# Two pairs of heads take turns in the products of probabilities and values

## The chip, the cores and the metric

One core of one Trainium2 chip runs the whole kernel in one launch. The metric is the device time of that launch in microseconds (us): 900.86 us is the median of 3 runs (900.86 to 901.72).

## The reference

Attention over 4 batches, 8 heads, 576 positions and a head dimension of 64, in float32, and then two gated layers. Heads 0 to 3 of each batch see the last 32 positions, heads 4 to 7 see every fourth of the last 128:

```python
scores = np.where(masks, scale * q @ k.T, -1e9)       # window 32, or 128 with step 4
attn = softmax(scores)
x = (attn @ v) as rows of 2304 tokens x 512           # 8 heads x 64
x = (sigmoid(x @ w_gate) * (x @ w_val)) @ w_out       # 512 -> 1536 -> 512
h = x @ w_in                                          # 512 -> 2048
out = (max(h, 0) + alpha * min(h, 0)) @ w_out2        # 2048 -> 512
```

## The kernel before, in words

**Blocks of heads.** The four heads of one kind in one batch make a block `hb` (0 to 7). They lie on the 128 partitions as two *pairs*: pair 0 on partitions 0 to 63, pair 1 on 64 to 127, 32 partitions for each head. The dilated heads are reordered by the host, so that both kinds become a band of windows of 32 positions: queries of window n need keys of windows n-1 and n.

**A product of probabilities and values** (`pv_mm`, L423 to L441) is computed for half of a block's 18 windows at a time. A matmul contracts over the 64 partitions of one pair: the weights are the values of one window (64 partitions x 128 columns, two heads beside each other), and what streams is the transposed probabilities of the one or two windows of queries that need them (64 or 32 columns). Both operands are split in a high and a low half in float16, and `passes` (L482) gives three matmuls for each window: high x high, high x low, low x high. The first half has 9 windows of keys, so 27 matmuls for each pair (24 with 64 columns and 3 with 32); the second half has 10, so 30 (24 and 6). Every matmul is compiled to a weight load of its own and the matmul. Each pair accumulates in a PSUM bank of its own, which `att_bank` gives. Block 0 takes another way (`pv32_mm`, L453, in float32, with 32 rows for each matmul), so seven blocks use `pv_mm`: 7 x 114 = 798 matmuls.

**What follows** is `pv_x` (L460): for each pair ScalarE reads the bank and writes the high half of `xh`, the input of the gate and value products, and VectorE writes the low half.

**Order of the work.** All instructions stand in an order written by hand, and each engine works through its own list in that order. The first batch, together with the decoding of the weights (VectorE, L179 to L187) and their powers of two (`total_of`, a matmul with one column, L148, then VectorE L156 and L160, then GpSimd L164), is a script of tasks, `FIRST`. In it `pvm hb half` is `pv_mm`, `pvx` is `pv_x`, `dec m` decodes, `wb m` bounds and `wsum m` sums a block of weights, `g b m` and `v b m` are the gate and value products (L590), `spl` splits weights. The parts around the first two uses are

```
pvm 1 1 4; pvm 1 0; dec 1; pvx 1 1 1; pvx 1 0 0; lgv 3; spl 0 1 1; pvx 1 1 0; g 0 0 0; wb 1; wsum 1; ... wpow 1
sig 0 7; pvm 2 0; wpow 9; v 0 7 1; spl 9 0; g 0 8 0; dec 10; ... pvx 2 0 0; ... g 0 8 1; wb 10; wsum 10
```

From then on a loop over batches runs the gate and value products of batch b (`gv_mm`, 12 blocks m of 128 columns) and its output products (`o1_mm`, L632), and `attention(b + 1)` hangs the next batch's attention on fixed places of that loop: block 2b at m = 7 and 8, block 2b + 1 in the output products (places 14 and 15). `prepare` fits the steps that prepare the second layer's weights (VectorE, ScalarE, GpSimd and transfers) between them. The gate and value products rotate through three buffers of two PSUM banks; ScalarE (L603) and VectorE (L608) empty them. After the attention comes the second layer (L964, L1207), whose weights went through memory in the meantime.

Of the kernel before, what the change touches and what calls it, by code (L numbers as in the profile page):

```python
# [17 lines left out]
WINDOW = 32  # L18
# [6 lines left out]
def attention_moe_kernel(  # L25
# [26 lines left out]
    H2 = S // 2  # L52
# [46 lines left out]
    def hold(bank, key):  # L99

        assert holds.get(bank) not in open_ and holds.get(bank) not in waiting, (bank, holds[bank], key)
        holds[bank] = key
# [18 lines left out]
    def att_bank(key, spare=None):  # L121
        if spare is None:
            turn["a"] = (turn["a"] + 1) % 2
            spare = 6 + turn["a"]
        hold(spare, key)
        waiting.add(key)
        return banks[:, spare, :]
# [264 lines left out]
    def pieces_of(hb):  # L392
        ends = [0, 352, 736, NB * 64] if hb < 2 else [0, NB * 64]
        return list(zip(ends[:-1], ends[1:]))

    def p_half(hb, z, c0, c1):
        for a, e in pieces_of(hb):
            if a <= c0 < e:
                assert c1 <= e
                o = 2 * a + z * (e - a) + c0 - a  # L400
                return st_[hb][0].bitcast(F16)[:, o:o + c1 - c0]
# [14 lines left out]
    xt = {}  # L416
    plain_v = set()

    def pv(hb, half):
        pv_mm(hb, half)  # L420
        pv_x(hb, half)

    def pv_mm(hb, half, spare=None):  # L423
        b, kind = divmod(hb, 2)
        v_ = vh[hb]
        first, last = (0, NB // 2) if half == 0 else (NB // 2, NB)
        ops = [(m, max(m, first), min(m + 2, last)) for m in range(max(first - 1, 0), last)]
        tiles = []
        for pair in range(2):
            k = slice(64 * pair, 64 * pair + 64)  # L430
            ps = att_bank(("pv", hb, half, pair), None if spare is None else spare + pair)[:, :H2]
            tiles.append(ps)
            for z, (m, n0, n1) in enumerate(ops):
                p_ = [p_half(hb, i, WINDOW * (m + n0 + 1), WINDOW * (m + n1 + 1))[k] for i in range(2)]
                w = [v_[k, i, m].rearrange("p h d -> p (h d)") for i in range(2)]
                for i, (a, x_) in enumerate(passes(w, p_)):
                    nc.tensor.matmul(  # L437
                        ps[:, WINDOW * (n0 - first):WINDOW * (n1 - first)], lhsT=a, rhs=x_,
                        start=(z == 0 and i == 0), stop=(z == len(ops) - 1 and i == 2), skip_group_check=True,
                    )  # L440
        xt[hb, half] = tiles  # L441

    def pv32_mm(hb, half, spare):

# [33 lines left out]
    def passes(w, x_):  # L478
        return ((w[0], x_[0]), (w[0], x_[1]), (w[1], x_[0]))
# [765 lines left out]
    def part(i):  # L1245
# [21 lines left out]
        "vhi": v_hi,  # L1267
        "vlo": v_lo,
        "pvm": pv_mm,
        "pv32": pv32_mm,  # L1270
        "pvx": pv_x,
# [33 lines left out]
    with tc.manual_schedule():  # L1305
# [66 lines left out]
        for n in range(2 * KD):  # L1372
            c, h = n // 2, n % 2
# [134 lines left out]
        i = 2 * turn["m"]  # L1508
# [169 lines left out]
```

## Time and profile before

| | us |
|---|---|
| median of 3 runs | 900.86 |
| the profiled execution, its own time | 900.97 |
| its span on the core | 899.2 |
| TensorE busy (matmuls) | 850.2 (95%) |
| VectorE busy | 681.9 (76%) |
| ScalarE busy | 450.4 (50%) |
| GpSimd busy | 304.6 (34%) |
| mean granted clock of TensorE | 0.967 of full speed |

The page of the profile gives busy times by engine, the span in 40 slices and the chain of work that ended last:

```profile
PE   7879789799999999999999989997899999999998
DVE  5999999825887767778695958678888888886751
PEclk9699689799999999999999999999999999999999
```

A digit is the busy share of one fortieth of the span (22.5 us) in tenths; PEclk is the granted clock in tenths. TensorE is busy throughout, but for the first eight slices, where VectorE is full, and a stretch after the middle. The 1.8 us by which the profiled time exceeds the span lie before the first and after the last instruction.

### The profile page before, as it was taken

The numbers are of one execution on the slowest core, as the hardware profiler recorded it, in microseconds if no ns is written. First come the engines' busy times: TensorE is split into PE (matmuls) and PEld (weight loads), VectorE is DVE, ScalarE is ACT, GpSimd is POOL, SyncE is SP. The second block draws the span as 40 slices with busy tenths as digits, with TensorE's granted clock in tenths as the row PEclk, the third lists the DMA queues.
The fourth block names the chain that finished last, engine by engine and source line by source line (L and its number), as shares of the span: only waits on it lengthen the run. The fifth ranks groups of instructions, "written<-read, shape, count | busy, mean of one in ns | idle before, by whom it ended". The sixth has DMA issues, their size and how long they took to land.

```text
span 899.2 us, 19438 instructions
## 1 busy us (share of the span) xinstructions
PE 850.2 (95%) x8196; PEld 701.5 (78%) x8196; DVE 681.9 (76%) x1039; ACT 450.4 (50%) x739; POOL 304.6 (34%) x264
## 2 busy tenths in 40 slices
PE   7879789799999999999999989997899999999998
PEld 5657567587787878777888768886788888888887
DVE  5999999825887767778695958678888888886751
ACT  4677556434453545343434556554565456545430
POOL 2456656600201101102024873245344454343220
PEclk9699689799999999999999999999999999999999
DMA  9764344104415425106756885954755685575462
GB/s 323 266 212 151 121 141 158 58 28 141 139 51 182 144 74 195 62 1 230 266 180 219 300 279 195 347 218 184 265 236 188 240 322 188 199 274 203 142 214 83
DMA packets 85176, 166.81 MB, mean 186 GB/s; under 512 B 5345, under 2 KB 57697, under 8 KB 85089
## 3 DMA queue, kind: packets, MB, share of 16 engines
q1 hardware_dynamic: 85088, 165.57, 52.5%
q8 instruction: 64, 1.05, 0.5%
q14 instruction: 24, 0.19, 0.1%
HBM read 137.24 MB, written 28.31 MB: 184 GB/s over the span
## 4 chain that ended last, share of the span: by engine, by line
PE 57%; DVE 26%; ACT 6%; issue 4%; DMA 4%; POOL 1%; SPq 1%; ACTq 0%; DVEq 0%; POOLq 0%
PE banks L590 14%; PE banks L1207 14%; PE banks L964 13%; PE banks L632 12%; DVE plain L183 4%; DVE plain L187 3%; PE banks L437 3%; DVE plain L179 2%; DVE temp_w L1010 2%; DVE temp_y L1010 1%; DVE gf L608 1%; DVE halves L824 1%; DMA words<-w_gate 1%; DVE g_gv L1049 1%; PE banks L323 1%
## 5 line engine op out<-in xcount | busy, mean ns | idle before, releaser
L590 PE MATMUL banks<-xh,w_gv 128*128 128x288 f16 x2304 | 297.7, 291 | 1.5 <-ACT sg L603 1.5
L590 PEld LDWEIGHTS <-w_gv 128*128 128x128 f16 x2304 | 226.1, 99 | 62.6 <-issue 1.8
L964 PE MATMUL banks<-yh,w_i 128*128 128x256 f16 x1536 | 189.9, 275 | 12.1 <-ACT temp_y L1019 6.4
L964 PEld LDWEIGHTS <-w_i 128*128 128x128 f16 x1536 | 151.3, 99 | 32.5 <-issue 12.3
L632 PE MATMUL banks<-gt,w_o 128*128 128x288 f16 x1152 | 149.5, 291 | 1.0 <-POOL gt L168 0.9
L632 PEld LDWEIGHTS <-w_o 128*128 128x128 f16 x1152 | 113.5, 100 | 31.9 <-issue 1.1
L1207 PEld LDWEIGHTS <-g_gv 128*128 128x128 f16 x780 | 76.7, 98 | 9.1
L1207 PE MATMUL banks<-w,g_gv 128*128 128x256 f16 x612 | 75.5, 273 | 0.0
L164 POOL TENSOR_SCALAR sc<-sc 128x1 f32<-128x1 f32 x35 | 12.4, 354 | 180.7 <-DVE sc L160 180.6
L1059 POOL TENSOR_TENSOR yh<-temp_y 128x512 f32<-128x512 f32 x16 | 27.0, 1689 | 131.6 <-DVE temp_y L1010 126.9
L194 ACT ACTIVATE junk<-plain 128x1024 bf16<-128x1024 f32 (+1 forms) x36 | 36.4, 1010 | 60.4 <-DVE plain L198 32.1
L1010 DVE SCALAR_TENSOR_TENSOR temp_w<-neg,sc,temp_w 128x256 f32<-128x256 f32 x48 | 55.5, 1195 | 10.9 <-ACT neg L1002 10.8
L187 DVE SCALAR_TENSOR_TENSOR plain<-words,plain 128x512 uint32<-128x512 uint32 x68 | 61.9, 931 | 1.2
L183 DVE SCALAR_TENSOR_TENSOR plain<-words,plain 128x512 uint32<-128x512 uint32 x68 | 59.3, 893 | 1.2
L1207 PEld LDWEIGHTS <-g_g 128*128 128x128 f16 x564 | 55.2, 98 | 6.4
L168 POOL TENSOR_TENSOR gt<-gf,gt 128x576 f16<-128x576 f32 x24 | 36.8, 1533 | 65.2 <-ACT gt L615 65.2
L608 DVE SCALAR_TENSOR_TENSOR gf<-banks,sg 128x576 f32<-128x576 f32 x48 | 36.0, 750 | 29.3 <-PE banks L590 28.9
L603 ACT ACTIVATE sg<-banks,sc 128x576 f32<-128x576 f32 x48 | 35.2, 734 | 35.1 <-PE banks L590 24.7
L615 ACT ACTIVATE gt<-gf 128x576 f16<-128x576 f32 x48 | 32.3, 675 | 38.3 <-DVE gf L608 38.3
L1207 PE MATMUL banks<-w,g_g 128*128 128x256 f16 x396 | 48.3, 273 | 0.0
L179 DVE TENSOR_SCALAR plain<-words 128x512 uint32<-128x512 uint32 x68 | 40.2, 612 | 8.9 <-DMA plain_dram<-plain 5.5
L388 POOL TENSOR_TENSOR s<-s,rs 128x1152 f32<-128x1152 f32 (+1 forms) x9 | 17.8, 1975 | 71.7 <-DVE rs L383 64.4
(170 smaller groups left out, 1300.1 us busy)
## 6 DMA issues: line engine op xcount, KB each, us to landing
w_i<-wi_dram SPq DMA_DIRECT2D x40, 896.0 KB, 6.4
w<-w_dram SPq DMA_DIRECT2D x52, 512.0 KB, 8.4
words<-w_out SPq DMA_DIRECT2D x28, 512.0 KB, 5.2
plain<-w_dram SPq DMA_DIRECT2D x18, 512.0 KB, 8.9
words<-w_in SPq DMA_DIRECT2D x16, 512.0 KB, 4.8
w_dram<-halves SPq DMA_DIRECT2D x28, 256.0 KB, 4.9
q<-qbd SPq DMA_DIRECT2D x6, 1152.0 KB, 6.5
words<-w_gate SPq DMA_DIRECT2D x12, 512.0 KB, 4.9
```

Source lines behind the costliest of these rows:

```text
L168: engine.tensor_tensor(out=lo, in0=src, in1=hi, op=ALU.subtract)
L179: nc.vector.tensor_scalar(out=d, in0=hi, scalar1=3, scalar2=0x3FFFFFFF, op0=ALU.logical_shift_left, op1=ALU.bitwise_and)
L183: nc.vector.scalar_tensor_tensor(out=d, in0=hi, scalar=0xC0000000, in1=d, op0=ALU.bitwise_and, op1=ALU.bitwise_or)
L187: nc.vector.scalar_tensor_tensor(out=d, in0=lo, scalar=29, in1=d, op0=ALU.logical_shift_right, op1=ALU.bitwise_or)
L194: nc.scalar.activation(junk[:, :src.shape[1]], src, AF.Square, accum_out=dst)
L590: nc.tensor.matmul(ps[:, h, :], lhsT=a, rhs=x_[:, H2 * h:H2 * h + H2], start=(kk == 0 and i == 0), stop=(kk == KD - 1 and i == 2),)
L603: nc.scalar.activation(halves(sg), ps, AF.Sigmoid, scale=sgx[b][:, m:m + 1])
L608: nc.vector.scalar_tensor_tensor(out=halves(gf), in0=ps, scalar=2.0 ** -15, in1=halves(sg), op0=ALU.mult, op1=ALU.mult)
L632: nc.tensor.matmul(ps[:, h, :], lhsT=a, rhs=x_[:, H2 * h:H2 * h + H2], start=(m == 0 and z == 0), stop=(m == M1 - 1 and z == 2),)
L964: nc.tensor.matmul(o, lhsT=h, rhs=l, start=(new and v == 0 and q == 1), stop=(q == total_), skip_group_check=True,)
L1010: nc.vector.scalar_tensor_tensor(out=temps[x_][:, c], in0=t[:, c], scalar=slope[:, u + v:u + v + 1], in1=src[:, c], op0=ALU.mult, op1=ALU.add,
L1207: nc.tensor.matmul(ps[:, H4 * t:H4 * t + H4].rearrange("p (c f) -> p c f", c=2), lhsT=a, rhs=x_, start=(first and k == 0 and t == 0 and z ...
```

## The change

Before, all matmuls of pair 0 of a half come first, then all of pair 1. After, the loop over pairs is the innermost: for each window and pass one matmul of pair 0 (rows 0 to 63 of the array) and then the same one of pair 1 (rows 64 to 127). Both banks are asked for at the start. The number, the operands and the order of the matmuls within a pair stay; so do the calls of `pv_mm` and of `pv_x`.

```diff
-        tiles = []
-        for pair in range(2):
-            k = slice(64 * pair, 64 * pair + 64)
-            ps = att_bank(("pv", hb, half, pair), None if spare is None else spare + pair)[:, :H2]
-            tiles.append(ps)
-            for z, (m, n0, n1) in enumerate(ops):
-                p_ = [p_half(hb, i, WINDOW * (m + n0 + 1), WINDOW * (m + n1 + 1))[k] for i in range(2)]
-                w = [v_[k, i, m].rearrange("p h d -> p (h d)") for i in range(2)]
-                for i, (a, x_) in enumerate(passes(w, p_)):
+        xt[hb, half] = [
+            att_bank(("pv", hb, half, pair), None if spare is None else spare + pair)[:, :H2] for pair in range(2)
+        ]
+        for z, (m, n0, n1) in enumerate(ops):
+            p_ = [p_half(hb, i, WINDOW * (m + n0 + 1), WINDOW * (m + n1 + 1)) for i in range(2)]
+            w = [v_[:, i, m].rearrange("p h d -> p (h d)") for i in range(2)]
+            for i, (a, x_) in enumerate(passes(w, p_)):
+                for pair, ps in enumerate(xt[hb, half]):
+                    k = slice(64 * pair, 64 * pair + 64)
                     nc.tensor.matmul(
-                        ps[:, WINDOW * (n0 - first):WINDOW * (n1 - first)], lhsT=a, rhs=x_,
+                        ps[:, WINDOW * (n0 - first):WINDOW * (n1 - first)], lhsT=a[k], rhs=x_[k],
                         start=(z == 0 and i == 0), stop=(z == len(ops) - 1 and i == 2), skip_group_check=True,
                     )
-        xt[hb, half] = tiles
```

## Rows read from the trace of the kernel before

**Rows 1.** The chain that ended last, page's part 4: shares of the span by engine

```profile
PE 57%; DVE 26%; ACT 6%; issue 4%; DMA 4%; POOL 1%; SPq 1%; ACTq 0%; DVEq 0%; POOLq 0%
```

**Rows 2.** Windows: stretch, length, busy (instructions) by engine, clock, DMA share, GB/s

```profile
0.00:175.35 175.35, 144.75 (x1482) 107.80 (x1482) 159.49 (x247) 106.92 (x193) 94.19 (x88) 0.86 0.55 183
175.35:437.80 262.45, 260.98 (x2759) 208.53 (x2760) 179.99 (x299) 118.61 (x170) 27.76 (x27) 0.99 0.35 118
```

**Rows 3.** All instructions of line 437: duration in ns, min/median/max

```profile
L437 PEld LDWEIGHTS <-vh x684: 92/95/129, 105.8 to 428.7; 64*128 64x128 f16 x171
L437 PE MATMUL banks<-s,vh x684: 172/190/239, 105.8 to 428.7; 64*128 64x64 f16 x150, 64*128 64x32 f16 x21
```

**Rows 4.** Windows of line 437 alone: PE, PEld busy, clock; four of 13 bursts

```profile
31.58:36.84 5.26, 5.26 (x112) 5.22 (x112) 0.50 0.91 303
...
105.77:108.46 2.69, 2.69 (x54) 2.65 (x54) 0.50 0.90 287
...
175.48:177.04 1.56, 1.56 (x54) 1.52 (x54) 1.00 0.05 11
...
427.14:428.85 1.71, 1.71 (x60) 1.67 (x60) 1.00 1.07 380
```

**Rows 5.** Timeline of PE, matmuls in flight in 116.60:116.70 and in 117.14:117.26

```profile
116.42 0.45 PE L437 MATMUL banks<-s,vh 64*128 64x64 f16 x10
...
116.97 0.46 PE L437 MATMUL banks<-s,vh 64*128 64x64 f16 x14
```

**Rows 6.** Timeline of PE, block 0's products, which alternate the pairs

```profile
16.82 2.12 PE L453 MATMUL banks<-pt,vc 32*64 32x64 f32 x72 [0.60 <-DVE mx L341]
```

**Rows 7.** Timeline of PE, one-column matmuls of L148; first and last of 23

```profile
461.19 0.24 PE L148 MATMUL banks<-sc,mask_sb 128*128 128x1 bf16 x4
...
461.75 0.16 PE L148 MATMUL banks<-mask_sb 128*128 128x1 bf16 x1
```

**Rows 8.** Timeline of PE, the first two matmuls of line 437

```profile
29.13 0.21 PE L437 MATMUL banks<-st_pt,second 64*128 64x32 f16 x2 [0.80 <-DVE xh L172]
```

**Rows 9.** Timelines of PE, DVE and POOL after block 1's products

```profile
36.84 3.06 PE L590 MATMUL banks<-xh,w_gv 128*128 128x288 f16 x12
...
38.03 0.81 DVE L172 SCALAR_TENSOR_TENSOR xh<-banks,xh 128x288 f16<-128x288 f32 x1
39.97 0.16 DVE L156 TENSOR_SCALAR sc<-banks 128x1 uint32<-128x1 uint32 x1 [1.13 <-PE banks L148]
...
34.05 1.64 POOL L168 TENSOR_TENSOR w_gv<-plain,w_gv 128x512 f16<-128x512 f32 x1 [1.45 <-ACT w_gv L205]
```

**Rows 10.** Timelines of PE and DVE after block 2's first half

```profile
108.46 6.41 PE L590 MATMUL banks<-xh,w_gv 128*128 128x288 f16 x36
...
114.96 0.16 DVE L156 TENSOR_SCALAR sc<-banks 128x1 uint32<-128x1 uint32 x1 [1.26 <-PE banks L148]
```

**Rows 11.** Timeline of PE after block 2's second half

```profile
130.76 0.48 PE L309 MATMUL banks<-mask_sb 128*128 128x384 bf16 x1 [3.83 <-DVE xh L172]
```

**Rows 12.** The chain in order of time: first and last of ten full-clock bursts

```profile
175.55 1.56 PE banks L437 x51
...
427.21 1.71 PE banks L437 x60
```

**Rows 13.** All of PE's waits in 175.4:437.8: total us, times, longest

```profile
PE banks L148 <- DVE sc L845: 2.5, 1, 2.5
PE banks L590 <- ACT sg L603: 1.5, 2, 1.2
```

**Rows 14.** Timeline of DVE: its last waits before the second layer's weights

```profile
447.83 0.43 DVE L179 TENSOR_SCALAR plain<-words 128x512 uint32<-128x512 uint32 x1 [3.26 <-DMA plain_dram<-plain]
...
461.49 0.76 DVE L608 SCALAR_TENSOR_TENSOR gf<-banks,sg 128x576 f32<-128x576 f32 x1 [0.26 <-PE banks L590]
```

**Rows 15.** Timeline of SP: transfers issued behind the last output product

```profile
439.16 0.34 SPq L652 DMA_DIRECT2D y_dram<-y  x1
```

**Rows 16.** Windows, as rows 2: the stretch behind block 3's first half

```profile
177.20:183.30 6.10, 6.10 (x40) 4.33 (x39) 1.44 (x2) 1.40 (x2) 0.00 (x0) 0.73 0.00 0
```

## The prediction

> **What bounds the kernel now.** I read the page's chain of waits first, then a table of windows by stage, then line 437 by itself, then timelines around each of its bursts. In the chain the reader is to see that TensorE holds 57% of it and VectorE 26% [rows 1]. The windows say where which one bounds. Up to 175.35 us VectorE is busy for 159.5 of 175.35 us and TensorE for 144.8; from there to 437.8 us TensorE is busy for 261.0 of 262.45 us and VectorE for 180.0 [rows 2]. The changed line has 13 bursts, one for each half of a block, save that block 1's two halves run as one behind a first two matmuls. Three of them lie in the first stretch (blocks 1 and 2), ten in the second (blocks 3 to 7), and all ten stand in the chain, the first and last as pieces of 1.56 and 1.71 us [rows 12]. So in the second stretch a microsecond taken from TensorE counts unless another engine falls behind; in the first it counts only as far as VectorE was waiting for it.
>
> **What one burst costs.** At full clock the burst of 54 takes 1.56 us and the one of 60 takes 1.71 us [rows 4]. The six more matmuls have 32 columns, so one of those costs 0.15 / 6 = 25 ns. Ten matmuls of 64 columns in flight start 0.45 - 0.19 = 0.26 us from first to last, nine steps of 29 ns [rows 3, 5]. One column in a cycle of 2.4 GHz would make 64 / 2.4 = 27 ns: the matmuls of one half of the rows already follow each other as fast as their columns stream, and the weight loads (busy beside them for 1.52 of the 1.56 us [rows 4]) cost nothing. No cost of loading goes away by the change; the only thing to gain is that two halves of the rows stream at once.
>
> **Do two halves stream at once?** The trace has a place where they do. In the middle of a burst the last three matmuls of pair 0 meet the first three of pair 1, all with 32 columns. There 14 matmuls start in 0.46 - 0.18 = 0.28 us [rows 5]. One after the other the 13 steps would be 7 x 29 + 6 x 25 = 353 ns. So some 73 ns are missing, three steps of 25 ns: three matmuls of one pair ran beside three of the other, each pair at its own step. Block 0's products alternate the same two halves, 32 rows at a time, and show no break between turns: 72 matmul records in 2.12 us, 29 ns each [rows 6].
>
> **The change part by part.** Nothing is added or removed: 798 loads and 798 matmuls stay, and no transfer moves. Block 1's opening needs the low half of the values for its third pass, as before; four matmuls instead of two go ahead of that wait. Both banks are needed at once, where pair 1's was needed half a burst later; its last reader is VectorE's `pv_x` of an earlier half, long past in every burst, so I cost that at nothing; if a bank were late, it would be by at most the 0.8 us that the half burst used to give. Pair 0's result used to be ready at half of the burst, and now is at the end of one that takes about half as long: nothing for `pv_x`.
>
> At full clock a burst of 54 becomes 27 steps: 24 x 29 + 3 x 25 = 771 ns. Before it was 48 x 29 + 6 x 25 - 75 = 1467 ns, and 1.56 us with the 0.09 us around it. The gain is 0.70 us. For 60: 24 x 29 + 6 x 25 = 846 ns against 1617 ns, a gain of 0.77 us. A block gains 1.47 us, and the five blocks in the second stretch 7.35 us. What may not pass this on: in that stretch TensorE waits for others for 2.5 us once, ahead of the first burst, and 1.5 us in two waits on ScalarE [rows 13]. The longer of these two is reached by a path over ScalarE and VectorE that itself starts at an earlier gate or value product, so it moves with TensorE. VectorE has 262.45 - 180.0 = 82 us idle there [rows 2], against 7 to take. Behind the stretch VectorE runs without idle time from 447.8 us, released by a transfer, to its 0.26 us wait for TensorE at 461.5 us [rows 14]. That would eat the gain if the transfer stood still; but transfers are issued in order, and SP sends the last output product first, at 439.2 us [rows 15], which TensorE finishes at 437.8. So it moves too. I count all 7.35 us.
>
> In the first stretch the clock is at half. Block 1 takes 5.26 us for 112 matmuls [rows 4]; half of it is 2.6 us saved on TensorE. Then come 12 gate products (3.06 us), the sum L148 and VectorE's reading of it at 39.97 us. VectorE was waiting for that for 1.13 us; without TensorE it would be ready at 38.03 + 0.81 = 38.84 us [rows 9]. TensorE's new date: the products need the low weights, which GpSimd ends at 34.05 + 1.64 = 35.69 us; four of the 12 don't, and eight at 0.255 us bring it to 37.7 us. VectorE is late next, and the gain is its 1.1 us. Block 2's first half takes 2.69 us at half clock [rows 4]: 1.3 us saved. 36 gate products in 6.41 us follow, and the sum for which VectorE waits 1.26 us [rows 10]. In these products the clock rises, about 3.5 us in (36 at 0.25 us, or at 0.124 us after the rise, make 6.2 us with 14 of the first kind). If it rises at the same time as before, five more of them run at half clock, 5 x 0.126 = 0.65 us; I count 0.65 us. Block 2's second half saves 0.77 us, which VectorE hides: the next thing of note on TensorE is 3.83 us of waiting for it [rows 11].
>
> The sum is 7.35 + 1.1 + 0.65 = 9.1 us. The profiled execution took 900.97 us by itself, so 891.9 us; against the median of 900.86 that is 9.0 us or 1.0%.
>
> **Bounds.** No row shows a long run of matmuls that alternate with 29 / 2 = 14.5 ns from start to start. The nearest from below is the meeting of the pairs (three steps hidden of three). From the other side are the one-column matmuls, 23 of them from 461.19 to 461.75 us, 25.5 ns each [rows 7], though these all use all rows. I take 14.5 ns, because the meeting is this very instruction on these halves. An exposed weight load is bounded by block 1's first two matmuls, which start 0.21 - 0.173 = 37 ns apart [rows 3, 8], 12 ns more than 25. The clock is one more term: after the idle time ahead of block 3 the next stretch ran at 0.73 of full speed for 6.1 us [rows 16], so 6.1 x 0.27 = 1.65 us were lost. Such a stretch may go or come where everything moves by some 2 us; I take none and keep 1.7 us either way.
>
> **Rivals.** *TensorE can't be fed that fast.* Matmul and load together are two instructions in 14.5 ns, and what ran so in the trace was short enough to have lain ready. If starts come 25 ns apart at best [rows 7], a burst of 54 takes 1.35 + 0.09 = 1.44 us and one of 60 takes 1.59: 0.12 us less in ten bursts, 1.2 us. Half clock is little touched (53 / 2 = 26.5 ns), so 1.75 us stay. 900.97 - 2.95 = 898.0 us. For it: no sustained row is faster than 25 ns. Against it: the meeting, which went at 12 ns for six matmuls. The Trainium skill, "TensorE: Matmul & The Clock Gate", section "Wait — 56ns, not 53.3ns?", states it as a rule, that starts never come closer than about 25 ns however few the columns are; by that rule the time is this rival's. The trace agrees for one set of rows (25.5 ns) and not where two halves met.
>
> *The gain is waited for elsewhere.* The halves overlap, but a path over ScalarE and VectorE that ends just behind TensorE takes its place, or they overlap already as far as they can. For it: VectorE's unbroken stretch [rows 14]. Against it: TensorE's waits of 1.5 us [rows 13], too few for another engine to be close behind in most bursts. About 900.5 us, nothing to be seen.
>
> *Slower: each turn exposes a weight load.* If a load can't run ahead when the next matmul is on the other half, and the halves don't stream at once, each matmul costs 12 ns more than its stream: 29 + 12 = 41 ns against a mean of 27. That is 14 ns x 570 = 8 us in the second stretch and about 2 us in the first, where 166 more stand on the path: 911 us. It decides as soon as the mean step is above 27 ns at full clock. Against it are the meeting and block 0's 29 ns [rows 5, 6].
>
> **How the numbers follow.** The forecast has a chance of 0.74, and its own range is 889.8 to 895 us: the clock's 1.7 us either way and up to 3 us that others take. The floor of 25 ns has 0.12, no change 0.08 and slower 0.06. The range of 889.8 to 898.4 us takes in the forecast and the floor and leaves out the other two and some of the forecast's tail. A measurement tells about 0.2% (1.8 us) from no change, and both of the first two cases lie beyond: faster 0.86, within 0.2% 0.08, slower 0.06.
>
> **What would show it.** In the changed profile a full-clock burst of 54 takes 0.86 us and one of 60 takes 0.94 us, about 20 matmuls are in flight in any 0.1 us of it, and the mean duration of one stays near 190 ns. VectorE's waits at L156 near 39 us and 114 us shrink, TensorE's waits between the first and last burst stay near 4 us, and the last burst ends some 9 us earlier. The floor shows as bursts of 1.4 us. The second rival shows as short bursts with new waits of TensorE at L590, or the same distance from the last burst to the end of the output products plus a longer wait behind. The slower one shows as bursts above 2 us. The forecast is wrong if bursts halve and the end moves by less than 6 us, or if they don't halve.

## The result, and the profile after

The changed kernel takes 893.21 us (median of 4 runs, 892.65 to 894.62) against 901.29 us for the kernel before beside it (4 runs, 900.86 to 901.96): a ratio of 0.9912 with a 95% interval of 0.9895 to 0.9929, so 0.9% faster. The forecast was 891.9 us. The profiled execution took 893.31 us, its span 891.5 us.

Lines behind the change have a number lower by one in the new kernel; line 437 is still the matmul. The engines' busy times, page's part 1, have 15.5 us less on TensorE and 2.5 us less on VectorE than before:

```profile
PE 834.7 (94%) x8196; PEld 686.4 (77%) x8196; DVE 679.4 (76%) x1039; ACT 449.0 (50%) x739; POOL 305.9 (34%) x264
```

Busy time taken away is not time gained: the span shrank by 7.7 us. Here are the windows of that line alone, seven of 13 bursts, as rows 4 before (start and end, length, PE and PEld busy, clock, DMA share, GB/s):

```profile
31.49:34.32 2.83, 2.83 (x110) 2.83 (x110) 0.50 1.05 359
104.40:105.90 1.50, 1.49 (x54) 1.44 (x54) 0.50 1.04 363
113.29:114.27 0.98, 0.97 (x60) 0.92 (x60) 1.00 0.73 245
173.21:174.69 1.48, 1.48 (x54) 1.44 (x54) 0.50 0.04 11
181.51:182.46 0.95, 0.95 (x60) 0.92 (x60) 1.00 0.00 0
246.24:247.15 0.91, 0.90 (x54) 0.84 (x54) 1.00 0.00 0
...
420.32:421.30 0.98, 0.97 (x60) 0.92 (x60) 1.00 0.97 281
```

The reader is to see pairs of equal clock: 5.26 became 2.83 us (with two matmuls more ahead of it), 2.69 became 1.50, 1.56 became 0.91 and 1.71 became 0.98 [rows 4] (each window ends where the next line begins, or a few hundredths later). And one burst ran at another clock than before: block 3's first half, at 173.21 us, ran at half clock, where before it ran at full.

The timeline of PE for 246.50 to 246.60 us says how many matmuls are in flight in a tenth of a microsecond, ten before [rows 5]:

```profile
246.31 0.46 PE L437 MATMUL banks<-s,vh 64*128 64x64 f16 x20
```

Twenty, each as long as it was (the median duration in the trace is 190 ns, as before [rows 3]). From first to last start it is 0.46 - 0.19 = 0.27 us for 19 steps, 14.2 ns each. That is a mean. The burst's single records in the trace start in twos, 3 to 4 ns apart, with 25 or 26 ns to the next two: each half keeps its own step of 29 ns, and the two run beside each other.

The two places where VectorE waited for TensorE in the first stretch, and the waits of TensorE from block 3 on (engine, line, for whom; us, times, longest):

```profile
38.57 0.20 DVE L156 TENSOR_SCALAR sc<-banks 128x1 uint32<-128x1 uint32 x1
...
112.27 0.14 DVE L156 TENSOR_SCALAR sc<-banks 128x1 uint32<-128x1 uint32 x1
```

```profile
PE banks L148 <- DVE sc L844: 3.5, 1, 3.5
PE banks L589 <- ACT sg L602: 1.5, 2, 1.2
PE banks L148 <- DVE xh L172: 0.6, 1, 0.6
```

VectorE's waits of 1.13 and 1.26 us [rows 9, 10] are gone. TensorE's wait ahead of block 3 grew from 2.5 to 3.5 us, the two waits on ScalarE stayed, and one of 0.6 us is new [rows 13].

Where the 7.7 us of the span came from can be read from the starts of TensorE's work in the two timelines:

| TensorE begins | before, us | after, us | moved by |
|---|---|---|---|
| block 2, first half | 105.77 | 104.41 | -1.36 |
| block 3, first half | 175.48 | 173.21 | -2.27 |
| block 3, second half | 183.28 | 181.51 | -1.77 |
| block 4, first half | 248.78 | 246.25 | -2.53 |
| block 4, second half | 256.33 | 253.11 | -3.22 |
| block 5, first half | 296.39 | 292.40 | -3.99 |
| block 5, second half | 306.88 | 302.21 | -4.67 |
| block 6, first half | 369.05 | 364.37 | -4.68 |
| block 6, second half | 376.59 | 371.23 | -5.36 |
| block 7, first half | 416.65 | 410.53 | -6.12 |
| block 7, second half | 427.14 | 420.33 | -6.81 |
| batch 3's first gate product | 437.68 | 430.11 | -7.57 |
| end of the span | 899.2 | 891.5 | -7.7 |

Each full-clock half moves what follows by 0.68 to 0.77 us. There are two exceptions. Block 3's two halves together gave 0.26 us, and block 5's second half gave nothing. From batch 3 on the distance stays in this trace. Over all ten traces of this document the time from batch 3's first gate product to the end of the span goes from 461.4 to 463.5 us, so a microsecond or two there is not the change's.

The chain of waits of the new kernel (shares of the span) has TensorE at 63% where it had 57%, and VectorE at 22% for 26% [rows 1]:

```profile
PE 63%; DVE 22%; ACT 5%; DMA 5%; issue 3%; POOL 1%; SPq 0%; ACTq 0%; DVEq 0%; POOLq 0%
```

### The profile page after: what moved, and what is told of

It reads as the page before. It is cut to its first block, busy times and chain, and to the rows that moved or that the text cites. A ratio compares the mean times of both kernels' runs of the same rounds, so it can differ in the third digit from the quotient of the medians.

```text
span 891.5 us, 19438 instructions
## 1 busy us (share of the span) xinstructions
PE 834.7 (94%) x8196; PEld 686.4 (77%) x8196; DVE 679.4 (76%) x1039; ACT 449.0 (50%) x739; POOL 305.9 (34%) x264
## 4 chain that ended last, share of the span: by engine, by line
PE 63%; DVE 22%; ACT 5%; DMA 5%; issue 3%; POOL 1%; SPq 0%; ACTq 0%; DVEq 0%; POOLq 0%
PE banks L1206 17%; PE banks L589 16%; PE banks L963 16%; PE banks L631 12%; DVE plain L183 4%; DVE plain L187 3%; DVE plain L179 3%; DVE halves L823 2%; DVE gf L607 1%; DMA w_dram<-halves 1%; PE banks L323 1%; DMA words<-w_gate 1%; DVE vh L282 1%; PE banks L437 1%; DMA words<-w_val 1%
## 5 line engine op out<-in xcount | busy, mean ns | idle before, releaser
L187 DVE SCALAR_TENSOR_TENSOR plain<-words,plain 128x512 uint32<-128x512 uint32 x68 | 59.7, 899 | 1.2
L183 DVE SCALAR_TENSOR_TENSOR plain<-words,plain 128x512 uint32<-128x512 uint32 x68 | 59.2, 892 | 1.2
```

What stands on the lines that cost most here:

```text
L183: nc.vector.scalar_tensor_tensor(out=d, in0=hi, scalar=0xC0000000, in1=d, op0=ALU.bitwise_and, op1=ALU.bitwise_or)
L187: nc.vector.scalar_tensor_tensor(out=d, in0=lo, scalar=29, in1=d, op0=ALU.logical_shift_right, op1=ALU.bitwise_or)
```

## The experiments

My theory was that the two halves of the rows stream at once, that a burst therefore halves, and that the end moves by what TensorE has on the path. Rivals were that the matmuls had been held by adding to the same columns one after the other, and that only a part of the path gains. Two smaller questions were where block 3's and block 5's share went.

**Is it the rows?** A control leaves the pairs apart, and makes the passes the outer loop, so that neighbours have different weights and share only 32 of their 64 columns (the edit in short):

```
         for pair in range(2):
-          for z in windows: for i in passes:
+          for i in passes: for z in windows:
```

> A control: the pairs stay apart as before the change, but within a pair the three passes are the outer loop, so that two matmuls in a row have different weights and write different columns of the bank. Theory (what the change gives is that the two halves of the rows stream at once): bursts stay at 1.56 and 1.71 us, about 901 us. Rival (the matmuls were held by three in a row that add to the same columns, and alternation spreads them): the step falls below 27 ns, bursts towards 0.9 us, 893 us.

One run took 900.51 us beside a median of 901.43 us before. The timeline of PE has the burst of block 4 in full:

```profile
246.58 1.62 PE L438 MATMUL banks<-s,vh 64*128 64x64 f16 x54
248.13 3.11 PE L590 MATMUL banks<-xh,w_gv 128*128 128x288 f16 x24
```

From its start to the next line's it is 1.55 us, as before, and in single records the step is still 28 to 30 ns. With one column in each cycle of 2.4 GHz, half of a matmul's columns now get their next addition some 16 ns later (29 - 32 / 2.4, an estimate), where it was 29 ns before, and nothing was held up by that. So the distance between two additions to the same columns is not what held the old order; the step stays, with the same rows at work. The control is read by its bursts and not by its time: its order also puts 20 matmuls of block 1 instead of 2 ahead of a wait, and its trace reaches block 3 at 173.42 us, 2.06 us earlier than before the change, with no two halves in turn.

One rival is left. The two pairs differ in their rows and also in their PSUM banks, and no run alternates banks on the same rows. That the rows count is argued from the step on the same rows, which goes with the clock: 53 to 54 ns between single records of block 1 at half clock and 29 ns at full, where 64 columns make 53 and 27 ns at one in each cycle.

**How far ahead does TensorE look?** Two kernels change turns less often, after three and after nine matmuls (the rest of the loop cut):

```
+        todo = [(z, i) for z in range(len(ops)) for i in range(3)]
+        for t in range(0, len(todo), 3):             # 9 in the second kernel
+            for pair in range(2):
+                for z, i in todo[t:t + 3]:
+                    ...
```

> The pairs change turns after every window, three matmuls each, not after each matmul. Theory (a matmul of the other half starts while up to three before it still wait, as where the pairs met in the kernel before): both halves stay filled, bursts of 0.86 and 0.94 us, and the time of the changed kernel, 893 us. Rival (matmuls start in the order of the program, one waiting holds all behind it): only the last of three meets the first of the next three, two steps of 29 ns in a turn, 18 x 58 = 1.04 + 0.09 = 1.13 us for 54; some 0.27 us less gain in each burst, about 3 us, 896 us.

> Turns of three windows, nine matmuls each. Theory (a look ahead of three): three of nine run beside the other half's, six steps in a turn, 6 x 6 x 29 ns + 3 x 29 + 0.09 us = 1.2 us for 54 matmuls; half of the gain, about 897 us. Rival, starts in the order of the program: eight steps in a turn, 1.5 us for 54, 900 us. Rival, a look ahead of nine or more: 0.86 us, 893 us.

Turns of three took 895.10 us (ratio 0.9933, 0.9917 to 0.9949), turns of nine 895.80 us (0.9942, 0.9927 to 0.9956), both against 901.62. The interval of turns of three overlaps with the changed kernel's, that of turns of nine hardly does, and the two overlap with each other, so the times order them poorly; the timelines of PE do it better. (In the trace of turns of three, batch 3's first gate product begins at 430.91 us, 6.8 us earlier than before the change, and 463.5 us follow, 2.1 us more than in the changed kernel, in a part that the edit doesn't touch.) Block 4's first half, in turns of three, and the product behind it:

```profile
247.02 0.95 PE L441 MATMUL banks<-s,vh 64*128 64x64 f16 x54
247.90 0.79 PE L593 MATMUL banks<-xh,w_gv 128*128 128x288 f16 x5
```

and in turns of nine:

```profile
247.06 1.23 PE L441 MATMUL banks<-s,vh 64*128 64x64 f16 x54
248.22 0.79 PE L593 MATMUL banks<-xh,w_gv 128*128 128x288 f16 x5
```

From one start to the next it is 0.88 us in turns of three, as when each matmul takes its turn (0.87 us, 292.40 to 293.27), and 1.16 us in turns of nine. Starts in the order of the program would have made these 1.13 and 1.5 us, an unlimited look ahead 0.86 both times, a look ahead of three matmuls 0.86 and 1.2. Single records of the turns of nine say the same. Six start one behind the other, 29 ns apart but for the first step, up to 247.215 us; the seventh start comes 9 ns later, and from there two trains of 29 ns run beside each other until the first has made its last three. Every change of turns in this burst looks like this. Read as the two halves, it says: where the next three matmuls are held up, the one of the other half behind them still starts, and none further back. It fits the old order, which had a meeting of just three [rows 5].

**Which part of the path gains?** One kernel alternates blocks 1 and 2 only, another blocks 3 to 7 only:

```
+        turn_len = 1 if hb < 3 else len(todo)        # hb > 2 in the other
```

> Blocks 1 and 2 alternate, blocks 3 to 7 stay as before. Theory (a burst halves, and the end moves by what TensorE's part of the path saves): the first stretch gives what it gave in the changed kernel's trace, 1.36 us behind block 1 and 0.72 us behind block 2, so 2.1 us, and the later bursts keep 1.56 and 1.71 us. Where the clock's half level falls ahead of block 3 may add or take 1.4 us: 898 to 901 us against 901.3. Rival (VectorE hides the first stretch): no change behind block 2.

> Blocks 3 to 7 alternate, blocks 1 and 2 stay as before. Theory: the part in which TensorE bounds gives 1.45 us for each of blocks 4, 6 and 7, 0.7 us for block 5 (its second half runs into a wait at L148), and block 3 gives its full 1.4 us if the clock ahead of it falls as it did before the change, or 0.4 us if as after it: 5.5 to 6.5 us, 894.8 to 895.8 us. Rival (the gain is lost where the path goes over other engines): under 4 us, above 897 us.

The back alone took 893.31 us (890.33 to 894.65; ratio 0.9909, 0.9885 to 0.9933), somewhat more of a gain than expected, and the whole change within its interval. Its trace has a span of 892.6 us and the second exception again: block 5's second half gave nothing. The first is not there: block 3 gave 1.83 us (its first half begins 0.21 us earlier than before the change, block 4's 2.04 us). Its first half ran at half clock, but what follows it at 0.86 of full speed (176.7 to 182.0 us). The front alone took 900.32 us of 901.62 (ratio 0.999, 0.998 to 1.0): at the edge of what can be told, and under the 2.1 us I expected. Its trace says what can happen to the first stretch. At 39 us it had the gain (VectorE at L156 at 38.43 us, against 38.57 in the changed kernel), and by 53 us it was gone. The kernels are alike up to block 3, so the difference lies between two executions. TensorE's 24 gate products took 4.14 us where the changed kernel's took 3.11. The timelines of PE and DVE of the front alone, and a line of POOL:

```profile
41.26 4.14 PE L593 MATMUL banks<-xh,w_gv 128*128 128x288 f16 x24
...
47.64 2.25 DVE L187 SCALAR_TENSOR_TENSOR plain<-words,plain 128x512 uint32<-128x512 uint32 x2
...
48.09 1.26 POOL L168 TENSOR_TENSOR w_gv<-plain,w_gv 128x512 f16<-128x512 f32 x1 [1.84 <-ACT w_gv L205]
```

and the same lines of the changed kernel:

```profile
40.85 3.11 PE L589 MATMUL banks<-xh,w_gv 128*128 128x288 f16 x24
...
47.27 1.28 DVE L187 SCALAR_TENSOR_TENSOR plain<-words,plain 128x512 uint32<-128x512 uint32 x2
...
48.23 1.34 POOL L168 TENSOR_TENSOR w_gv<-plain,w_gv 128x512 f16<-128x512 f32 x1 [2.36 <-ACT w_gv L205]
```

The granted clock was 0.75 of full speed from 41.3 to 45.5 us in the one and full from 40 to 45 us in the other. The sum behind the products came later against the rest, and VectorE's two L187 took 2.25 instead of 1.28 us while GpSimd worked beside the second one (here GpSimd began first, at 48.09 against 48.2 us, in the changed kernel the second L187 did). Turns of three have the same in their trace: 3.92 us for the products, 2.25 us for the two L187. That GpSimd's work lengthened VectorE's is argued from the coincidence and was not tried by itself. The rival (VectorE hides the first stretch) held in some executions and not in others. VectorE reads the next sum at L156 at 51.44 us in the kernel before. Of the seven traces in which block 1 takes turns, five have it at 49.89 to 50.11 us, the front alone and turns of three at 51.36 and 51.40 us.

**Block 3 and the clock.** In the changed kernel's first trace TensorE waits 3.5 us for alpha's sum on VectorE, and block 3's first half comes behind it. I ran the changed kernel again, and a kernel in which TensorE does block 3's first half and the 36 products behind it ahead of that sum:

```
-alpha; pvm 3 0; o 0 2 0; o 0 2 1; pvx 3 0 1;
+pvm 3 0; o 0 2 0; o 0 2 1; alpha; pvx 3 0 1;
```

> The changed kernel once more, beside the others on the same chip: 893 us, 0.991 of the kernel before.

> The changed kernel, with block 3's first half and the 36 output products behind it placed ahead of alpha's sum on TensorE, which waits 3.5 us for VectorE there. Theory (block 3 gave 0.45 us instead of 1.47 because this wait stands ahead of it and the clock was at half behind it): TensorE works through the wait, the span shrinks by 3 to 4 us, 889.5 us against 893.2. Rival (VectorE sets the pace past 175 us and what moves ahead is waited for at the next sum): less than 1 us, 892.5 us.

The changed kernel took 892.99 us (5 runs, 891.34 to 894.85; ratio 0.991, 0.9894 to 0.9925). Its new trace answers the question by itself. The windows from block 3's first half to its second, with the clock behind the five engines' busy times, in the first trace:

```profile
173.20:181.50 8.30, 8.30 (x95) 6.15 (x93) 1.90 (x5) 2.21 (x4) 0.21 (x1) 0.63 0.01 2
```

and in the second:

```profile
173.70:179.10 5.40, 5.40 (x95) 4.47 (x93) 1.91 (x5) 1.94 (x4) 0.21 (x1) 1.00 0.01 3
```

The same 95 records took 8.3 us at 0.63 of full speed and 5.4 us at full speed. TensorE's wait ahead of them was 2.5 us in the second trace, as in the kernel before:

```profile
173.58 0.18 PE L148 MATMUL banks<-sc,mask_sb 128*128 128x1 bf16 x1 [2.51 <-DVE sc L844]
```

At 437.7 us the second trace is 9.9 us ahead of the kernel before, where the first was 7.6 us ahead. So block 3's missing share was the clock, and it comes and goes with the execution: block 3 gave 0.26 us in the first trace (0.45 stands in the expectation of the kernel with the sum moved) and 3.1 us in the second, where the 1.65 us came back that the kernel before lost there [rows 16]. That the idle TensorE brings the clock down is argued, from all ten traces. Eight have a wait of 2.5 to 3.7 us ahead of block 3, and seven of them ran a part of this stretch at half clock; the two that have no wait there ran it at full clock. Against it: in the kernel before the clock fell only behind block 3's first half, not in the wait.

With the sum moved the time is 889.46 us (ratio 0.9867, 0.9852 to 0.9882), beyond the changed kernel's interval. In its timeline of PE the wait of 3.5 us is gone; 1.5 us of it come back ahead of the second half:

```profile
169.84 0.94 PE L437 MATMUL banks<-s,vh 64*128 64x64 f16 x54
170.71 4.58 PE L631 MATMUL banks<-gt,w_o 128*128 128x288 f16 x36
...
177.29 1.02 PE L437 MATMUL banks<-s,vh 64*128 64x32 f16 x60 [1.49 <-DVE sc L156]
```

**Block 5's second half.** A sum at L148 stands 12 output products behind it and uses a corner of pair 0's bank, so it needs VectorE's low half of pair 0. In the changed kernel:

```profile
303.15 1.64 PE L631 MATMUL banks<-gt,w_o 128*128 128x288 f16 x12
305.44 0.16 PE L148 MATMUL banks<-sc,mask_sb 128*128 128x1 bf16 x1 [0.64 <-DVE xh L172]
```

ScalarE's timeline in the same kernel:

```profile
302.31 0.74 ACT L649 ACTIVATE y<-banks,sc 128x576 f32<-128x576 f32 x1 [5.96 <-PE banks L631]
...
303.77 1.43 ACT L171 ACTIVATE xh<-banks 128x288 f16<-128x288 f32 x2
```

It copies the finished output product and bounds it before it comes to the high halves of the values at 303.77 us. That path starts with the end of the previous output product (302.2 us), not with the values, so it did not get shorter, while TensorE's did. One kernel lets the sum come six products later, on top of the edit before:

```
-                    if m in (2, 6, 10):
+                    if m in ((3, 6, 10) if d == KD - 1 else (2, 6, 10)):
```

> As the run before it, and the preparation step in the last block of output products comes one block of six matmuls later, behind 18 matmuls instead of 12. Theory (block 5's second half lost its 0.76 us to a wait of 0.64 us at L148 for VectorE's low half of pair 0): this wait goes, 0.6 us more, 889 us. Rival (the wait moves to the next reader of that bank): no more than the run before it.

It took 889.95 us (ratio 0.9873, 0.9858 to 0.9888), no better as a time than the kernel without it: 0.6 us can't be told. In its timeline of PE the wait is gone:

```profile
298.96 2.38 PE L631 MATMUL banks<-gt,w_o 128*128 128x288 f16 x18
301.25 0.16 PE L148 MATMUL banks<-sc,mask_sb 128*128 128x1 bf16 x1
```

Batch 3's first gate product begins 0.75 us earlier than in the kernel before it (425.14 against 425.89 us). Both kernels beat the one before the change and the changed one.

## Why the prediction was right, point by point

- **The step of a burst.** Predicted 0.86 and 0.94 us at full clock and about 20 matmuls in flight; measured 0.87 (292.40 to 293.27) and 0.95, and 20. The choice of 14.5 ns, from a meeting of three matmuls, held as a mean for bursts of 60. The rival of a floor of 25 ns fell, and with it the slower one: no load became exposed. The Trainium skill's rule of 25 ns from start to start ("TensorE: Matmul & The Clock Gate", section "Wait — 56ns, not 53.3ns?") holds in this case for matmuls on the same rows (25.5 ns [rows 7]) and not for two halves in turn (14.2 ns in the mean).
- **Half clock.** Predicted 1.3 and 2.6 us saved for TensorE; measured 1.2 and 2.4.
- **The first stretch.** Predicted 1.1 + 0.65 us on the path; the profiled execution has 1.36 and, at VectorE's sum behind block 2's second half, 0.71 more. Behind block 1 VectorE was late next, as said. Behind block 2 the number came out right by luck. I had the clock rise at the same time as before; it rose earlier, and the 36 products took 5.43 us instead of 6.41 [rows 10]. VectorE read the sum behind them at 112.27 instead of 114.96 us, 1.33 us more than the 1.36 it had, and lost 0.62 us of this again by 118.86 us, with two L187 of 2.24 instead of 1.28 us:

```profile
105.88 5.43 PE L589 MATMUL banks<-xh,w_gv 128*128 128x288 f16 x36
...
114.73 2.24 DVE L187 SCALAR_TENSOR_TENSOR plain<-words,plain 128x512 uint32<-128x512 uint32 x2
```

The clock can do this without the change: in the back alone block 2 takes no turns, but its first half ran at 0.72 of full speed instead of 0.50, and VectorE reads this sum at 113.50 us without a wait. And two executions lost nearly all of block 1's gain again by 53 us; the front alone is worth 1.3 us in medians. I took this stretch as settled by one execution, and it isn't.
- **The second stretch.** Predicted 7.35 us; from 173.21 to 430.11 us the first trace has 7.57 - 2.27 = 5.3 us. There the term was too large, by 2 us, and two steps of it were mis-sized. Block 3's 1.47 us was 0.26 us, since the clock fell ahead of it; I had allowed 1.7 us for this and taken none. Block 5's second half, 0.77 us, went into a wait of 0.64 us. There the step that failed is "the gain passes on, because VectorE has 82 us idle": what counts is not idle time over the stretch but the one path over ScalarE and VectorE that ended together with TensorE. The second rival named this; it cost one half of ten. The second trace of the same kernel has 9.92 - 1.77 = 8.15 us in this stretch, and the back alone 7.08 - 0.21 = 6.87 us. So the clock's term, which the sum took at nothing, moved the gain by nearly 3 us between two executions, and 7.35 us lies among them.
- **Behind the stretch.** I said that transfers and VectorE move with TensorE. Batch 3's products begin 7.57 us earlier, and the span ends 7.7 us earlier.

The range held the time, and its upper part was there for the right reasons, the clock and other engines' paths. That the profiled execution came within 1.5 us of the forecast is in part luck: the front gave 2.27 us where 1.75 were counted, the back 5.3 where 7.35 were.

## What to carry to other kernels

In this kernel matmuls with a contraction of 64 rows cost little more than half (1.56 to 0.87 us) when the two halves of the rows take turns, since their columns, not their loads, set the step; a burst in turns of three is nearly as short (0.88 us). What such a gain is worth is read from the path: for each place where TensorE gets faster, look up the next instruction that waits for another engine, and what that engine's chain starts with. And where TensorE stands idle, put work that is ready there, since the clock of what follows may fall too, as it did behind block 3's wait in seven traces of eight.

## What the runs showed that I had not expected

Two executions of the same program on the same data differ by microseconds, and most by the clock: block 3's 95 records took 5.4 or 8.3 us in two executions of one kernel, and its lead over the kernel before at 437.7 us was 9.9 or 7.6 us. And matmuls don't start strictly in the order of the program here: in turns of nine, 54 of them took 1.16 us, between the 0.87 us of perfect overlap and the 1.5 us of starts in order, and single records show three matmuls being passed at each change of turns.
